# A chunked scan feeding a two-layer network: other places for weight loads, rows, pairs, dummies and state decay

## The chip, the cores and the metric

The kernel runs on one core of a Trainium2 chip. A core has five engines that run side by side and wait for one another through semaphores: TensorE (PE, matrix products into PSUM), VectorE (DVE), ScalarE (ACT), GpSimd (POOL) and SyncE (SP), which here issues every DMA. Each engine works through its own instructions in the order in which the program gives them. The metric is the device time of one execution in microseconds (us), smaller is better.

## The reference, cut to what matters

Two stages are computed: a gated linear scan over the sequence (batch 4, 8 heads, 768 positions, head size 32, state size 16), and a network of two layers over all 3072 tokens (256 to 2048 to 256, leaky ReLU between).

```python
for c in range(nc):                                   # chunks
    cum = np.cumsum(la, axis=-1)                      # la = log of the clipped gate a
    L = np.exp(cum[:, :, :, None] - cum[:, :, None, :]) * causal
    M = np.einsum('bhin,bhjn->bhij', Cc, Bc) * L
    y = np.einsum('bhij,bhjd->bhid', M, xc) \
        + np.einsum('bhin,bhnd->bhid', Cc, state) * np.exp(cum)[..., None]
    Bx = np.einsum('bhjn,bhjd->bhjnd', Bc, xc) * decay_from_j[..., None, None]
    state = decay_full * state + Bx.sum(2)
...
h = x @ w_in                                          # x: all y, tokens by heads * head size
out = np.maximum(0.01 * h, h) @ w_out
```

The weights come in double precision and are turned into a high and a low part of single precision on the chip.

## The kernel before, in words

The scan is cut into chunks of 96 positions (the result does not depend on the chunk length). One chunk of one batch element is a unit; there are 32 units, u = 4 c + b for chunk c and batch element b.

**The prelude** loads the gates `la`, takes the logarithm, and forms cumulative sums on PE: `split_sums` gives the sums as rows (`crow`, and in three bf16 parts, `parts`), `columns` gives them as columns. Both row forms go to DRAM. `keep_warm` (L112 to 117) issues matmuls of a zero tile, the dummies: 3 at the start. The decay matrix `lt` of units 0 and 1 is made directly: `decay_mask` (L226 to 231) writes a mask into PSUM, `decay_direct` adds the sums, `decay_of` takes the exponential. `dl` and `dr` are tiles of constants and of loaded parts from which `decay_pe` makes the decay of units 2 to 15 by one matmul pair each; two memsets (L146, L147) and fills prepare them.

**The first stage** (loop at L596) runs units 0 to 15, one after another: `scores` of the next unit (L301, with one dummy ahead), `unit_out` (L378: the products of the unit, L330, and its new state, L339, then copies by ACT and POOL), `decay_pe` two units ahead, and DVE's subtract `rest`. `bns[c]` are the state operands of a chunk; `state_decay(c)` (L291) multiplies them on POOL with the decay and has to come before L339 of the chunk's first unit. It is issued at the end of the last unit (b = 3) of the chunk before. From unit 3 on each unit also does one pass of the decode of the weights.

**The decode.** A weight tile f of 16 is fetched to one of three buffers `raw` (`fetch_w`, L90), then five passes: `decode_hold`, `decode_shift`, `do_sign`, `do_low` on DVE (L425, L431, L438, L445) and, from tile 3 on, `decode_rest` (L458; for the first three tiles POOL does it, L480). ACT takes the absolute value at the beginning (L420) and makes the high part at the end (L451). `do_low(f)` is the last reader of the raw tile; it issues the load of tile f + 3 right behind itself, and that load waits for it.

**The second stage** (loop at L831) has 64 steps. In step s PE multiplies a block of 512 tokens with a tile of the first weights (`ffn_in`, L517, six matmuls), ACT applies the nonlinearity twice (L524 into `gh`, L527 in place), DVE subtracts (`ffn_low`, L530, into `gl`), and three steps later PE multiplies with the second weights (`ffn_out`, L541, twelve matmuls in two banks). `hp` has two banks, so `ffn_in` of step s waits for `gl` of step s - 2. `PASSES` says how many decode passes follow in each step.

The other 16 units run in pairs at the steps of `PAIR`: `pair_block` (L382) has the products of the pair before and the scores of the new one. Their decay goes another way: `decay_rows` (L269) loads the sums from DRAM (`crow_d`) to all partitions of `lt`, `decay_sub` (L276) subtracts on POOL, `decay_exp` (L283) takes the exponential on ACT and a causal select on POOL. The dictionary `early` holds what a step issues ahead of all else: rows four steps before the pair, subtracts three and two, exponentials two and one, the state decay one. `lt` has four buffers, so the rows of a pair wait for the products of the pair before.

**The third stage** (`two_tiles`, L762) does the last two token blocks together with seven products in place of eight. `COMBINE` is the step at which its operands begin to be formed, `LAST_OUT` the step of the last scan products.

What sets the order is the program text alone: each engine and SP's DMA queue do their instructions in that order, and a waiting instruction holds up all behind it.

Of the kernel before, what the change touches and what calls it, by code (L numbers as in the profile page):

```python
# [17 lines left out]
NB, NH, S, D, N = 4, 8, 768, 32, 16  # L18
Q = 96
# [10 lines left out]
C_COLS = NB * 2 * Q  # L30
BC_COLS = B_COLS + C_COLS
LAG = 3
WARM = 3
RAWS = 3
SHIFT = 448
LOAD = 4
# [11 lines left out]
DIRECT = 2  # L48
SLOTS = 8

PAIR = {16: 7, 18: 13, 20: 20, 22: 31, 24: 36, 26: 41, 28: 46, 30: 51}
LAST_OUT = 56
COMBINE = 57

PASSES = (3,) * 12 + (2,) * 20
KD = Q + 3 * NH + 3
MAG_MIN = float(np.uint32(0x38000000).view(np.float32))
MAG_MAX = float(np.uint32(0x47EFFFFF).view(np.float32))
# [3 lines left out]
def scan_ffn(ctx: ExitStack, tc: tile.TileContext, a_l, bc_l, bn_l, x_l, w_l, out_l):  # L62
# [27 lines left out]
    def fetch_w(f, eng=nc.sync):  # L90
        raws[f] = wr.tile([128, 2 * DM, 2], U32, name="raw")
        eng.dma_start(raws[f].rearrange("p c w -> p (c w)"), w_l[f].bitcast(U32))
# [50 lines left out]
    nc.vector.memset(later, 0.0)  # L143
    nc.vector.memset(after, 1.0)
    nc.vector.memset(less, -1.0)
    nc.vector.memset(dl[Q:], 1.0)  # L146
    nc.vector.memset(dl[Q:Q + 3 * NH, :, Q:], 0.0)  # L147
    nc.gpsimd.affine_select(
        out=upto[:, :Q], in_=upto[:, :Q], pattern=[[1, Q]], compare_op=ALU.is_ge,
        fill=0.0, base=0, channel_multiplier=-1,  # L150
# [18 lines left out]
    def fill_first():  # L169
        nc.vector.tensor_copy(dr[:Q, 0], later.unsqueeze(1).to_broadcast([Q, NH, Q]))  # L170
# [36 lines left out]
    def split_sums(prow):  # L207
        for g in range(2):
            nc.tensor.matmul(
                prow[:, g], lhsT=la[:, g * 128:(g + 1) * 128], rhs=upto[:, :Q],  # L210
                start=True, stop=True,
            )
        nc.scalar.copy(crow, prow)
        nc.vector.tensor_copy(parts[:, :, 0], prow)
        nc.vector.tensor_tensor(out=rest, in0=prow, in1=parts[:, :, 0], op=ALU.subtract)
        nc.vector.tensor_copy(parts[:, :, 1], rest)
        nc.vector.tensor_tensor(
            out=parts[:, :, 2], in0=rest, in1=parts[:, :, 1], op=ALU.subtract
        )
# [6 lines left out]
    def decay_mask(space):  # L226
        for g in range(2):
            nc.tensor.matmul(
                heads_of(space, g), lhsT=upto_b,
                rhs=later.unsqueeze(1).to_broadcast([Q, NH // 2, Q]), start=True, stop=False,  # L230
            )
# [230 lines left out]


    passes = collections.deque()

    def settle(f=None):
        for g in list(pending) if f is None else [f] * (f in pending):
# [15 lines left out]
    def do_low(f):  # L483
        decode_low(f)
        defer(decode_high, f)
        if f < POOLED:
            defer(rest_pool, f)
        if f + RAWS < NF:
            fetch_w(f + RAWS)

    for f in range(NF):
        passes.append((decode_hold, f))
# [67 lines left out]
    with tc.tile_pool(name="ps_d", bufs=2, space=PSUM, reuse_waits="tile") as ps_d:  # L560

        def free_tile():
            return ps_d.tile([128, 2, TS], F32, name="pd")

        fill_first()
        nc.vector.tensor_scalar(
            out=la, in0=la, scalar1=1e-6, scalar2=1.0, op0=ALU.max, op1=ALU.min,
        )
        nc.scalar.activation(la, la, AF.Ln)
        pds = [free_tile() for _ in range(2)]  # L570
        second = score_tile()
        for u in range(DIRECT):
            fill_reach(u)
            decay_mask(pds[u])
        fill_less()
        split_sums(first[:, 0, :2 * Q].rearrange("p (g i) -> p g i", g=2))
        nc.sync.dma_start(parts_d.rearrange("(g r) t i -> r g t i", g=2), parts)
        decay_load(DIRECT, SLOTS)
        nc.sync.dma_start(crow_d.rearrange("(g p) i -> p g i", g=2), crow)
        columns(erev, after, AF.Exp, second[:, 0])  # L580
        state_decay(0)
        nc.scalar.copy(dl[:Q], upto_b.unsqueeze(1).to_broadcast([Q, SLOTS, QE]))
        fill_slots(1, SLOTS // 2)
        decay_direct(0, pds[0])
        decay_of(0, pds[0])
        fetch_bc(1)
        fetch_w(0)
        fetch_x(1)
        fetch_bn(1)
        fetch_w(1)  # L590
        fetch_x(2)
        scores(0)
        fill_slots(SLOTS // 2, SLOTS)
        decay_direct(1, pds[1])
        decay_of(1, pds[1])
        for u in range(FIRST_UNITS):  # L596
            if u == FIRST_UNITS - 1:
                settle()
                leads.close()
                pg = ctx.enter_context(tc.tile_pool(name="pg", bufs=LAG + 2))  # L600
                pob = ctx.enter_context(tc.tile_pool(name="pob", bufs=3))
                ffn_in(0, free_tile()[:, 0])
                ffn_act(0)
            if u + 1 < FIRST_UNITS:
                scores(u + 1, 1, u == 5)
            rest = unit_out(u, free_tile())
            v = u + 2
            if v < FIRST_UNITS:
                decay_pe(v, free_tile())
            rest()  # L610
            c, b = divmod(u, NB)
            if c + 2 <= FIRST_UNITS // NB:
                if b == 0 and c:
                    alloc_x(c + 2)
                    fetch_x(c + 2)
                if b == 2:
                    fetch_bc(c + 2)
                    if c == 0:
                        fetch_w(2)
                if b == 3:  # L620
                    fetch_bn(c + 2)
            if b == 3 and c + 1 < FIRST_UNITS // NB:
                state_decay(c + 1)
            if u == 2:
                decode_abs(0)
            if u > 2 and u < FIRST_UNITS - 1:
                decode(1)
            if u > 4:
                settle()
        ffn_low(0)  # L630
        ffn_in(1, score_tile()[:, 0])

    ps_o = ctx.enter_context(tc.tile_pool(name="ps_o", bufs=2, space=PSUM, reuse_waits="tile"))
# [9 lines left out]
    for u, b in PAIR.items():  # L643
        pair_at[b] = ((u - 2, u - 1) if u > FIRST_UNITS else (), (u, u + 1))
        for e in range(2):
            at(early, b - 4, decay_rows, u + e)
            at(early, b - 3 + e, decay_sub, u + e)
            at(early, b - 2 + e, decay_exp, u + e)
    pair_at[LAST_OUT] = ((NU - 2, NU - 1), ())
# [181 lines left out]
    for s in range(total):  # L831
        for f, args in early.get(s, ()):
            f(*args)
        n = PASSES[s] if s < len(PASSES) else 2
        if s >= AHEAD:
            ffn_in(s)
        if s:
            ffn_act(s)
        settle()
        if s:  # L840
            ffn_low(s)
        if s in pair_at:
            pair_block(*pair_at[s])
        decode(n)
        if s == COMBINE:
            open_two()
            sums(0)
            sums_split(0)
            temps = [su.tile([128, 2, TS], F32, name=n) for n in ("t12", "t34")]
            combining = combine(TWO, (px, bx, px, px), temps, rhs)  # L850
        if combining:
            next(combining, None)
        if s >= LAG:
            outs_due.append(s - LAG)
        if rested or not outs_due or steps[outs_due[0]] not in firsts or outs_due[0] == 0:
            while outs_due:
                ffn_out(outs_due.popleft())
            rested = False
        else:
            rested = True  # L860
# [48 lines left out]
```

## Time and profile before

| | |
|---|---|
| Median of 3 runs | 352.66 us (349.25 to 355.47) |
| The profiled execution | 354.02 us, its span from the first to the last instruction 352.3 us |
| Prelude and first stage | 0 to about 58 us of the span |
| Second stage | about 58 to 259 us |
| Third stage | about 259 us to the end |

Times in the profile count from the start of the span. A row of the timeline gives the start, the length, the engine, the line of the kernel, the operation, the tiles (out, then in), shapes and the count; in brackets stands how long the engine was idle before it and what ended that time. Of rows with several instructions the length is from the first start to the last end. "SPq" is the time of SP's DMA issues, "issue" is waiting that the profile puts down to nothing. Rows of the chain of work that ended last give start, length, engine, tile, line and count. Rows of windows give a stretch, its length, and the busy time and count of PE, PE's weight loads, DVE, ACT and POOL, then the granted clock, the DMA share and GB/s.

### The profile page before, as it was taken

The page shows a single profiled execution, that of the slowest core. Times are in us where ns is not written, and L with a number is a line of the kernel's source. Part 1 is how long each engine was busy: PE and PEld are TensorE (multiplying, and loading weights), DVE is VectorE, ACT ScalarE, POOL GpSimd, SP SyncE. Part 2 cuts the span into 40 slices and gives each one's busy share as a digit, 9 for nine tenths or more (in the row PEclk, how much of TensorE's full clock was granted, in tenths as well). Part 3 has the DMA queues.
Part 4 walks back from the last instruction along what each step waited for, and adds up shares of the span by engine and source line. Part 5 has one row for each costly group of instructions (what it writes and reads, how often), then busy time and mean ns, then how long its engine had stood idle before and what let it go on. Part 6 is the DMA issues. An engine that isn't in the chain of part 4 may idle for free.

```text
span 352.3 us, 6257 instructions
## 1 busy us (share of the span) xinstructions
PE 329.3 (93%) x2410; PEld 252.2 (72%) x2410; DVE 206.9 (59%) x344; ACT 182.4 (52%) x354; POOL 124.4 (35%) x213
## 2 busy tenths in 40 slices
PE   8997978959699999999998999999999999999995
PEld 4554546738578778888886888788887777778774
DVE  5467557769476589443343432526747866676652
ACT  4365437475454466363526545345637564545651
POOL 4157455060340351043525445204206544466100
PEclk9999689969969999999999999999999999999999
DMA  4797321715711471011056120100001000000003
GB/s 153 223 278 213 110 97 61 219 38 188 211 62 61 139 243 40 0 37 45 0 177 180 66 79 2 61 0 0 2 0 60 2 0 0 0 3 1 0 2 119
DMA packets 10555, 27.94 MB, mean 79 GB/s; under 512 B 2109, under 2 KB 2461, under 8 KB 10525
## 3 DMA queue, kind: packets, MB, share of 16 engines
q1 hardware_dynamic: 10525, 27.54, 24.7%
q8 instruction: 19, 0.31, 0.4%
q14 instruction: 11, 0.09, 0.1%
HBM read 24.14 MB, written 3.39 MB: 78 GB/s over the span
## 4 chain that ended last, share of the span: by engine, by line
PE 72%; DVE 9%; DMA 6%; POOL 4%; issue 4%; ACT 3%; SPq 1%; POOLq 0%; ACTq 0%; DVEq 0%
PE hp L517 19%; PE op L541 19%; PE sc L723 8%; DMA lt<-crow_d 6%; PE sc L742 6%; PE op L742 3%; PE hp L723 3%; PE sc L394 2%; PE sc L311 2%; PE sc L330 2%; PE pd L330 2%; POOL lt L277 2%; DVE u L803 2%; DVE c L804 2%; PE pd L254 2%
## 5 line engine op out<-in xcount | busy, mean ns | idle before, releaser
L530 DVE TENSOR_TENSOR gl<-hp,gh 128x512 fp32r<-128x512 f32 x62 | 42.7, 689 | 81.7 <-ACT hp L527 81.6
L524 ACT ACTIVATE gh<-hp 128x512 fp32r<-128x512 f32 x62 | 36.8, 594 | 63.3 <-PE hp L517 63.2
L517 PE MATMUL hp<-xh,wh 128*128 128x512 f32 x124 | 50.0, 403 | 9.8 <-DVE gl L530 9.8
L541 PE MATMUL op<-gh,wh 128*128 128x512 f32 x128 | 51.0, 399 | 0.0
L541 PE MATMUL op<-gh,wl 128*128 128x512 f32 x128 | 49.9, 390 | 0.0
L541 PE MATMUL op<-gl,wh 128*128 128x512 f32 x128 | 49.8, 389 | 0.0
L517 PE MATMUL hp<-xl,wh 128*128 128x512 f32 x124 | 49.3, 397 | 0.0
L517 PE MATMUL hp<-xh,wl 128*128 128x512 f32 x124 | 49.2, 397 | 0.0
L366 POOL COPY xs<-stage 16x64 f32<-16x64 f32 x112 | 29.6, 264 | 42.3 <-ACT stage L363 31.3
L277 POOL TENSOR_TENSOR lt<-lt,ccol 112x768 f32<-112x768 f32 x16 | 23.5, 1469 | 51.4 <-DMA lt<-crow_d 51.3
L527 ACT ACTIVATE hp<-hp 128x512 f32<-128x512 f32 x62 | 36.7, 593 | 0.0
L517 PEld LDWEIGHTS hp<-xh,wh 128*128 128x128 f32 x124 | 23.8, 192 | 17.0 <-DVE gl L530 10.5
L689 POOL TENSOR_TENSOR sl<-s,sh 128x512 fp32r<-128x512 f32 x8 | 10.4, 1300 | 67.7 <-ACT sh L688 67.7
L541 PEld LDWEIGHTS op<-gh,wh 128*128 128x128 f32 x128 | 24.1, 188 | 7.1 <-issue 1.2
L286 POOL TENSOR_SCALAR_AFFINE_SELECT lt<-lt 96x768 f32<-96x768 f32 x16 | 14.7, 916 | 38.4 <-ACT lt L285 38.4
L541 PEld LDWEIGHTS op<-gl,wh 128*128 128x128 f32 x128 | 24.0, 188 | 5.2
L541 PEld LDWEIGHTS op<-gh,wl 128*128 128x128 f32 x128 | 24.2, 189 | 4.7
L517 PEld LDWEIGHTS hp<-xl,wh 128*128 128x128 f32 x124 | 23.8, 192 | 5.1
L517 PEld LDWEIGHTS hp<-xh,wl 128*128 128x128 f32 x124 | 23.9, 192 | 4.7
L285 ACT ACTIVATE lt<-lt 112x768 f32<-112x768 f32 x16 | 13.5, 842 | 23.5 <-POOL lt L277 23.5
L755 DVE TENSOR_TENSOR gl<-c,gh 128x512 fp32r<-128x512 f32 x24 | 24.4, 1038 | 1.4 <-ACT c L752 1.1
L751 ACT ACTIVATE gh<-c 128x512 fp32r<-128x512 f32 x24 | 15.1, 627 | 14.6 <-DVE c L804 9.1
(161 smaller groups left out, 633.8 us busy)
## 6 DMA issues: line engine op xcount, KB each, us to landing
raw<-w_l SPq DMA_DIRECT2D x16, 512.0 KB, 3.7
lt<-crow_d SPq DMA_DIRECT2D x16, 336.0 KB, 4.9
bc<-bc_l SPq DMA_DIRECT2D x8, 608.0 KB, 4.3
xs<-x_l SPq DMA_DIRECT2D x8, 384.0 KB, 7.1
out_l<-ob SPq DMA_DIRECT2D x12, 256.0 KB, 2.0
bn<-bn_l SPq DMA_DIRECT2D x8, 231.0 KB, 6.5
parts_d<-parts SPq DMA_DIRECT2D x1, 144.0 KB, 1.9
la<-a_l SPq DMA_DIRECT2D x1, 96.0 KB
```

The source lines that it names most:

```text
L277: nc.gpsimd.tensor_tensor(out=lts[u], in0=lts[u], in1=ccol[:, u * NH:(u + 1) * NH].unsqueeze(2).to_broadcast([QE, NH, Q]), op=ALU.subtract,)
L286: nc.gpsimd.affine_select(out=lt[:Q], in_=lt[:Q], pattern=[[0, NH], [1, Q]], compare_op=ALU.is_ge, fill=0.0, base=0, channel_multiplier=-1,)
L366: nc.gpsimd.tensor_copy(to[:, :, hh], stage[hh * D:hh * D + N])
L517: nc.tensor.matmul(hp, lhsT=w_half[half][:, f, k * 128:(k + 1) * 128], rhs=x[t][:, k, :], start=(n == 0), stop=(n == 5),)
L524: nc.scalar.activation(ghs[s], hp, AF.Prelu, alpha=0.01)
L527: nc.scalar.activation(hps[s], hps[s], AF.Prelu, alpha=0.01)
L530: nc.vector.tensor_tensor(out=gls[s], in0=hps.pop(s), in1=ghs[s], op=ALU.subtract)
L541: nc.tensor.matmul(op, lhsT=w_half[half][:, f, DM + m * 128:DM + (m + 1) * 128], rhs=x, start=(first and i == 0), stop=(last and i == 2),)
L723: nc.tensor.matmul(bank, lhsT=w[h], rhs=x[g], start=start and i == 0, stop=i == 2, skip_group_check=True,)
L742: nc.tensor.matmul(outs[t][m], lhsT=w_half[half][:, f, DM + m * 128:DM + (m + 1) * 128], rhs=x, start=first and i == 0, stop=last and i == 2,)
L751: nc.scalar.activation(gh, h, AF.Prelu, alpha=0.01)
L755: nc.vector.tensor_tensor(out=gl, in0=g, in1=gh, op=ALU.subtract)
```

## The change

- Weight loads: `do_low` only notes the tile; the noted loads are issued at the head of the next step (behind what `early` issues), or, in the first stage, at the end of the next unit ahead of that unit's decode pass.
- Pairs: the steps become 6, 12, 18, ... 48 (before 7, 13, 20, 31, 36, 41, 46, 51), the last products 54 (56), the combining 56 (57). Rows are loaded five steps ahead of a pair (four).
- Passes: three for 14 steps (12), but one at a step with a pair.
- Dummies: six at the start (three), two after the sums; none ahead of the scores in unit 0.
- State decay of chunk c + 1 after the third unit of chunk c (after the fourth).
- The prelude: the two memsets of `dl` move behind the sums, the fill of `dr` behind the direct reach, the masks behind the columns; the state operands of chunk 1 are fetched ahead of its x.
- In unit 0 the products come ahead of the scores of unit 1; in unit 15 `ffn_low(0)` comes right behind `ffn_act(0)`.

```diff
-WARM = 3
+WARM = 6
+WARM2 = 2
...
-PAIR = {16: 7, 18: 13, 20: 20, 22: 31, 24: 36, 26: 41, 28: 46, 30: 51}
-LAST_OUT = 56
-COMBINE = 57
-
-PASSES = (3,) * 12 + (2,) * 20
+PAIR = {16: 6, 18: 12, 20: 18, 22: 24, 24: 30, 26: 36, 28: 42, 30: 48}
+LAST_OUT = 54
+COMBINE = 56
+
+PASSES = (3,) * 14 + (2,) * 20
...
-    nc.vector.memset(dl[Q:], 1.0)
-    nc.vector.memset(dl[Q:Q + 3 * NH, :, Q:], 0.0)
...
     passes = collections.deque()
+    fetches = collections.deque()
+
+    def fetch_more():
+        while fetches:
+            fetch_w(fetches.popleft())
...
         if f + RAWS < NF:
-            fetch_w(f + RAWS)
+            fetches.append(f + RAWS)
...
-        fill_first()
...
         for u in range(DIRECT):
             fill_reach(u)
-            decay_mask(pds[u])
+        fill_first()
         fill_less()
         split_sums(first[:, 0, :2 * Q].rearrange("p (g i) -> p g i", g=2))
+        nc.vector.memset(dl[Q:], 1.0)
+        nc.vector.memset(dl[Q:Q + 3 * NH, :, Q:], 0.0)
...
         columns(erev, after, AF.Exp, second[:, 0])
+        for u in range(DIRECT):
+            decay_mask(pds[u])
+        keep_warm(second[:, 1], WARM2)
         state_decay(0)
...
         fetch_w(0)
+        fetch_bn(1)
         fetch_x(1)
-        fetch_bn(1)
...
                 ffn_act(0)
+                ffn_low(0)
+            if u == 0:
+                rest = unit_out(u, free_tile())
             if u + 1 < FIRST_UNITS:
-                scores(u + 1, 1, u == 5)
-            rest = unit_out(u, free_tile())
+                scores(u + 1, int(u > 0), u == 5)
+            if u:
+                rest = unit_out(u, free_tile())
...
-            if b == 3 and c + 1 < FIRST_UNITS // NB:
+            if b == 2 and c + 1 < FIRST_UNITS // NB:
                 state_decay(c + 1)
+            fetch_more()
...
-        ffn_low(0)
         ffn_in(1, score_tile()[:, 0])
...
-            at(early, b - 4, decay_rows, u + e)
+            at(early, b - 5, decay_rows, u + e)
...
         for f, args in early.get(s, ()):
             f(*args)
-        n = PASSES[s] if s < len(PASSES) else 2
+        fetch_more()
+        n = 1 if s in pair_at else PASSES[s] if s < len(PASSES) else 2
```

## The prediction, made before the changed kernel had run

> **What bounds the kernel now.** I read the page first, then the list of idle stretches of TensorE (PE), then the timeline around each, then who waited for whom on the queues.
>
> ```profile
> span 352.3 us, 6257 instructions
> ...
> PE 329.3 (93%) x2410; PEld 252.2 (72%) x2410; DVE 206.9 (59%) x344; ACT 182.4 (52%) x354; POOL 124.4 (35%) x213
> ...
> PEclk9999689969969999999999999999999999999999
> ```
>
> PE is the bound, and by its share of busy time there seems to be nothing left to win. The clock row says otherwise: in three places the granted clock falls to 0.6 or 0.8, so part of the 329.3 busy us is the same work done slowly. All three follow an idle stretch. The first two stretches lie in the first stage (16 units of the scan, one chunk of four units after another). Each row below is the score matmul that opens a unit, from the timeline of PE:
>
> ```profile
> 29.83 0.74 PE L311 MATMUL sc<-bc 32*112 32x192 f32 x8
> 31.77 0.59 PE L311 MATMUL sc<-bc 32*112 32x192 f32 x8
> ...
> 35.26 0.44 PE L339 MATMUL pd<-xs,bn 112*32 112x32 f32 x16 [2.42 <-POOL bn L292]
> ...
> 36.88 1.00 PE L311 MATMUL sc<-bc 32*112 32x192 f32 x8
> ...
> 40.06 1.00 PE L311 MATMUL sc<-bc 32*112 32x192 f32 x8
> ...
> 42.58 0.59 PE L311 MATMUL sc<-bc 32*112 32x192 f32 x8
> ...
> 44.84 0.74 PE L311 MATMUL sc<-bc 32*112 32x192 f32 x8
> ...
> 50.09 1.00 PE L311 MATMUL sc<-bc 32*112 32x192 f32 x8
> ...
> 52.70 0.59 PE L311 MATMUL sc<-bc 32*112 32x192 f32 x8
> ```
>
> An undisturbed unit takes 31.77 - 29.83 = 1.94 us. The unit from 31.77 takes 5.11, because the state matmul L339 waits for POOL's state decay L292, which stands behind POOL's other work of the unit before. The next two take 3.18 and 2.52: the same eight score matmuls need 1.00 us instead of 0.59, so the clock has fallen. The pattern repeats at 44.84 (5.25, then 2.61).
>
> In the second stage (steps of the feed-forward, with a scan pair every few steps) PE idles four times for over 0.7 us near a pair, and the queues tell why:
>
> ```profile
> 74.24 0.80 PE L517 MATMUL hp<-xh,wh 128*128 128x512 f32 x1 [4.41 <-DVE gl L530]
> 96.91 0.80 PE L517 MATMUL hp<-xh,wh 128*128 128x512 f32 x1 [2.72 <-DVE gl L530]
> 123.37 0.50 PE L517 MATMUL hp<-xh,wh 128*128 128x512 f32 x1 [0.77 <-DVE gl L530]
> 188.19 0.50 PE L517 MATMUL hp<-xh,wh 128*128 128x512 f32 x1 [0.95 <-DVE gl L530]
> ```
> ```profile
> 65.01 0.85 SPq L272 DMA_DIRECT2D lt<-crow_d x2
> 70.14 1.47 POOL L277 TENSOR_TENSOR lt<-lt,ccol 112x768 f32<-112x768 f32 x1 [11.25 <-DMA lt<-crow_d]
> 71.64 0.84 ACT L285 ACTIVATE lt<-lt 112x768 f32<-112x768 f32 x1 [4.89 <-POOL lt L277]
> ```
> ```profile
> SPq L92 <- DVE w L445: 75.5, 13, 10.6
> ```
>
> Read these from the bottom up. SP sends transfers in program order. A weight load L92 waits on SP until DVE has finished the decode pass that frees its buffer, 75.5 us in all, and whatever stands behind it waits too. So the rows L272 of the first pair leave only at 65.01 and land just ahead of POOL's subtract at 70.14; ACT, in order too, sits 4.89 us before the exponential L285 with the activations of the next step behind it; DVE gets no gl; PE gets no free bank and idles 4.41 us. PE names DVE, but the cause is the place of a DMA in SP's queue.
>
> **The change, part by part.**
>
> *State decay one unit sooner (b == 2).* The decay of chunks 1 to 3 moves ahead of one unit's four POOL copies and, for chunks 2 and 3, of one weight subtract.
>
> ```profile
> L292 POOL TENSOR_TENSOR bn<-bn,erev x7: 1052/1055/1060, 6.8 to 170.8; 112x512 f32<-112x512 f32 x7
> ```
>
> Its 1.05 us must then end within a unit and a half before L339 needs it. It could wait for its own transfer: behind it on POOL would stand the copies of the next unit, which nothing reads for four units. I take both stalls as gone. The five units above took 5.11 + 3.18 + 2.52 + 5.25 + 2.61 = 18.67 us. With no stall each costs between 1.94 and 2.26 (42.58 to 44.84, with a short wait in it); DVE has a decode pass in each, so I take 2.1: 18.67 - 10.5 = **8.2 us won** (ends 7.4 and 9.0).
>
> *Rows at b - 5, weight loads issued at the head of the next step, pairs every six steps.* Rows now go out one step after the pair before (the earliest at which their buffer is free) and stand ahead of the step's weight load in SP's queue, not behind it. For the first pair they are emitted two steps sooner, directly behind the load of the last first-stage decode.
>
> ```profile
> DMA to landing us min/median/max: 4.0/4.9/7.3
> ```
> ```profile
> 81.95 1.36 PE hp L517 x6
> ...
> 126.08 0.86 PE sc L394 x16
> ```
>
> (The first row is for L272.) A step is two groups of six matmuls, 2 x 1.36 = 2.72 us. From a pair's matmuls to the exponential four steps on lie more than three steps, 8.2 us; the longest landing of 7.3 and a subtract of 1.47 make 8.8, and the two banks of hp give about a step more. So all four idle stretches should go: 4.41 + 2.72 + 0.77 + 0.95 = **8.85 us won**. The slow clock behind the first two goes with them:
>
> ```profile
> 74.24 2.93 PE hp L517 x6
> 77.17 1.58 PE sc L394 x16
> 78.75 3.20 PE op L541 x12
> ...
> 96.91 2.93 PE hp L517 x6
> ...
> 101.70 1.57 PE sc L394 x16
> ```
>
> First: (2.93 - 1.36) + (1.58 - 0.86) + (3.20 - 2.72) = 2.77. Second: 1.57 + 0.71 = 2.28. Together **5.05 us won**; the work of a pair itself is not less, only placed elsewhere. The weight load a step later costs SP nothing by itself: SP runs ahead of the engines and was waiting for the same decode pass anyway, so the load leaves when that pass ends, unless the rows ahead of it wait (for the products of the pair before, past by then). What is late next is DVE. The first fourteen steps have three decode passes (one where a pair stands), and two early pairs fall among them; POOL's subtract then runs beside DVE:
>
> ```profile
> 62.50 0.68 DVE L458 TENSOR_TENSOR wl<-w,wh 128x512 fp32r<-128x512 f32 x1
> ...
> 134.44 1.74 DVE L458 TENSOR_TENSOR wl<-w,wh 128x512 fp32r<-128x512 f32 x1
> ```
> ```profile
> 80.00:94.00 14.00, 14.00 (x63) 11.41 (x61) 10.92 (x21) 5.91 (x11) 1.19 (x1) 1.00 0.74 240
> ```
>
> With almost no POOL work DVE is busy 10.92 of 14.00 us at three passes, and one pass stretched by 1.06 us beside POOL's subtract. Two pairs with two subtracts each give 4 x 1.06 = 4.2 us of DVE time; between 0 and 4.2 of it reaches PE, and I take **2 us lost**. (The Trainium skill, "SBUF — State Buffer", Who interferes with whom, says that a DVE instruction with two SBUF inputs is blocked for the whole of a GpSimd instruction that reads SBUF. By that rule each subtract could hold DVE for its full 1.47 us, 5.9 in all; the trace shows 1.06 at the worst place I found.)
>
> *gl of step 0 moved into unit 15.* In the trace PE waits for it:
>
> ```profile
> 58.61 0.47 PE L517 MATMUL hp<-xh,wh 128*128 128x512 f32 x1 [0.97 <-DVE gl L530]
> ```
>
> It now goes ahead of the unit's own subtract on DVE. **0.5 won** (0 to 0.97).
>
> *The prelude: three dummies more at the start, two before the decay of chunk 0, masks behind the sums, no dummy in unit 0.*
>
> ```profile
> 1.06 1.46 PE L114 MATMUL sc<-idle 128*128 128x512 bf16 x3 [1.06 <-DVE idle L110]
> 3.08 1.53 PE L228 MATMUL pd<-later,upto_b 96*112 96x384 bf16 x4 [0.56 <-DVE upto_b L192]
> 6.08 2.77 PE L235 MATMUL pd<-lt,after 96*112 96x384 f32 x4
> 14.90 0.89 PE L254 MATMUL pd<-dr,dl 123*112 123x384 bf16 x2
> 17.99 0.53 PE L254 MATMUL pd<-dr,dl 123*112 123x384 bf16 x2
> ```
>
> Six dummies at 1.46 / 3 = 0.49 end near 4.0, in time that PE spent on the masks or idle, so they cost nothing. The four mask matmuls (1.53) lay in the shadow of the logarithm and now stand on PE's path, with 2 x 0.49 of dummies; one dummy goes (0.5), and the sums start perhaps 0.4 sooner: 1.53 + 0.98 - 0.5 - 0.4 = 1.6 later at the slow clock, half of that if the clock rises at the same time. I take **1.2 lost**. The ends are 3.3 lost (the rise falls a stretch of slow clock later as well) and about 4 won (second rival). The moved memsets and fills of DVE and the swapped transfers bn and x of chunk 1 have later readers and count zero; cover gone, they cost their own length, under 1 us each. An end of the scan two steps sooner, combining one step sooner: zero, as the third stage waits for none of it.
>
> **Sum:** -8.2 - 8.85 - 5.05 - 0.5 + 2 + 1.2 = -19.4. The profiled execution took 354.02 us around its span of 352.3, which gives 334.6; it stands 1.36 above the median of 352.66, from which the sum gives 333.3. The slow stretches differ between executions and most of them should go, so I also count a little for what I left out (the slow products at the second stall): **333 us**.
>
> **The rivals.**
>
> 1. *One pair still stalls, or DVE becomes the bound.* For it: DVE's 78% at three passes, before POOL's share; the loads of a chunk now share DMA with rows and weights. Against: the median landings. One stall as large as the first keeps 4.41 + 2.77 = 7.2: 340. All 4.2 us of the stretched passes: 335 to 336.
>
> 2. *The dummies raise the clock early.* If the clock rises near 8 instead of between 14.90 and 17.99, ten us of slow work halve at most; ScalarE and DVE between the units leave some 4: 333 - 1.2 - 4 = 328. Against:
>
> ```profile
> 3.08:14.90 11.82, 11.82 (x67) 6.49 (x67) 6.56 (x12) 4.50 (x7) 2.76 (x3) 1.00 0.56 181
> ```
>
> PE is busy for all 11.82 us from 3.08 on, and still the two L254 matmuls take 0.89 at 14.90 and 0.53 only at 17.99; the long fp32 matmuls (L235) seem not to count as full activity, and they stay behind the dummies. The Trainium skill, "TensorE: Matmul & The Clock Gate", Part 1, gives some 3.4 us of sustained work as enough, in a free-running window. Taken plainly that rule speaks for this rival, but the trace does not agree with it here, as 11.82 us without a gap did not do.
>
> 3. *The pairs do not move off the path.* If the rows are held by something other than the weight loads, the second stage keeps its 13.9 us: 347, about no change.
>
> 4. *Slower: weights arrive late.* Ten weight tiles are loaded in the loop. Behind rows and a chunk's transfers each may land late, ACT's absolute value of the tile waits, and the activations wait behind it, as they did for L285.
>
> ```profile
> DMA to landing us min/median/max: 3.1/3.7/9.7
> ```
>
> Between the pass that frees a buffer and the pass that needs its next tile lie nine passes and three gl on DVE, 12 x 10.92 / 21 = 6.2 us. At the median of 3.7 it is 2.5 early; at 9.7 it would be 3.5 late. To end over 2% slower all ten would have to cost (19.4 + 7) / 10 = 2.6 us, so nearly every landing beyond 8.8. Nothing in the trace comes near that.
>
> **How the numbers follow.** 329 to 337 us, as forecast: 0.45. Second rival, 325 to 329: 0.13; below that 0.02. First rival, 337 to 342: 0.22. Between this and the third (342 to 347): 0.10. Other small gains or none, to 359: 0.05. Fourth rival, beyond 359.7: 0.03. From 325 to 342 lie 0.80. Two per cent, about what a measurement of this kernel can tell from no change, is 7 us: faster than 345.6 is 0.89 (0.07 of the 0.10), within 0.08, slower 0.03.
>
> **What would show it.** Right: no L339 waiting for L292 over 0.5 us, and units near 2.1 us up to the feed-forward; no fall of the clock after the prelude; L272 issued right after a pair's products; no gl wait on PE over 1 us. The prelude's step is wrong if the L254 of unit 2 or earlier takes 0.53. The forecast is wrong if PE still waits for gl near the first two pairs, with L285 waiting for L277 (rows late), or with DVE busy without a gap (DVE the bound), or with the absolute value L420 waiting for a weight transfer (fourth rival).

## The result, and the profile after

| | median | runs | lowest to highest |
|---|---|---|---|
| Before (beside the changed kernel) | 352.54 us | 11 | 350.90 to 356.68 |
| Changed | 333.58 us | 5 | 332.60 to 333.99 |

The ratio is 0.9462, with a 95% interval of 0.9438 to 0.9486: 19.0 us less. An earlier set of four runs gave a ratio of 0.9506 (0.9361 to 0.9652), in which one execution of 788.77 us does not count. Every matmul of the feed-forward is twice as long there; it stands in the last section, and the profile after shown here is of another execution (332.69 us, span 331.0).

The page of the changed kernel:

```profile
span 331.0 us, 6272 instructions
...
PE 315.6 (95%) x2414; PEld 244.3 (74%) x2414; DVE 217.1 (66%) x344; ACT 182.9 (55%) x354; POOL 126.6 (38%) x213
...
PEclk9999999999999999999999999999999999999999
```

PE is busy 13.7 us less although it has four more matmuls: the clock no longer falls. This is not peculiar to the two profiles: the mean granted clock was 0.969 to 0.984 in the eleven executions of before and 0.993 to 1.000 in the five of the changed kernel. To see where the rest went, set the starts of the units against those of before. First one row of before, then the timeline of PE after (start, length, engine, line, tiles, and in brackets the wait ahead):

```profile
16.15 1.00 PE L311 MATMUL sc<-bc 32*112 32x192 f32 x8
```
```profile
12.19 0.50 PE L254 MATMUL pd<-dr,dl 123*112 123x384 bf16 x2 [1.33 <-DMA dr<-parts_d]
12.85 0.59 PE L311 MATMUL sc<-bc 32*112 32x192 f32 x8
...
29.06 0.59 PE L311 MATMUL sc<-bc 32*112 32x192 f32 x8
...
32.15 0.38 PE L116 MATMUL sc<-idle 128*128 128x512 bf16 x1 [1.18 <-DVE lt L318]
32.46 0.74 PE L311 MATMUL sc<-bc 32*112 32x192 f32 x8
...
36.19 0.74 PE L311 MATMUL sc<-bc 32*112 32x192 f32 x8
...
38.46 0.74 PE L311 MATMUL sc<-bc 32*112 32x192 f32 x8
...
40.91 0.38 PE L116 MATMUL sc<-idle 128*128 128x512 bf16 x1 [0.65 <-DVE lt L318]
...
43.16 0.59 PE L311 MATMUL sc<-bc 32*112 32x192 f32 x8
...
48.36 0.51 PE L522 MATMUL hp<-xh,wh 128*128 128x512 f32 x1 [0.25 <-DVE gl L535]
...
56.36 0.50 PE L522 MATMUL hp<-xh,wh 128*128 128x512 f32 x1 [0.59 <-DVE gl L535]
...
63.86 0.50 PE L522 MATMUL hp<-xh,wh 128*128 128x512 f32 x1 [2.26 <-DVE gl L535]
```

The first row of L311 here is unit 2, then come units 9, 10, 12, 13 and 15. With the rows of before in the prediction this gives, stage by stage:

| stretch | before | after | difference |
|---|---|---|---|
| start to the scores of unit 2 | 16.15 | 12.85 | -3.30 |
| units 2 to 8 | 15.62 | 16.21 | +0.59 |
| the five units that held both state-decay stalls (9 to 11, 13, 14) | 18.67 | 7.13 + 4.70 = 11.83 | -6.84 |
| unit 12 | 2.26 | 2.27 | +0.01 |
| unit 15 to the feed-forward | 5.91 | 5.20 | -0.71 |
| second stage | 205.74 | 194.64 | -11.10 |
| third stage | 87.95 | 88.0 | 0 |

The second stage is read from windows (the stretch and its length, then the busy time and count of PE, PE's weight loads, DVE, ACT, POOL, the granted clock, the DMA share, GB/s), of before and of after:

```profile
58.61:264.35 205.74, 196.88 (x1341) 158.33 (x1341) 116.09 (x192) 105.81 (x207) 61.43 (x95) 0.97 0.25 79
```
```profile
48.36:63.86 15.50, 12.63 (x65) 9.41 (x65) 14.88 (x22) 11.59 (x22) 7.28 (x8) 1.00 0.48 154
63.86:243.00 179.14, 179.14 (x1277) 145.28 (x1277) 110.98 (x172) 95.36 (x187) 57.01 (x89) 1.00 0.25 79
```

(A step has six matmuls of L522 and six of L546, two times three; a row with twelve of them spans two steps.) Before, PE was idle for 205.74 - 196.88 = 8.86 us. After, it is idle for 2.87, all in the first 15.5 us, and from 63.86 on it does not stop once in 179 us. The other 5.11 us (196.88 - 12.63 - 179.14) are the same count of matmuls (1341) done at a fuller clock, 0.97 before and 1.00 after. The two profiles differ by 21.3 us and the medians by 19.0: the profile of before stands 1.5 above its median here, that of after 0.9 below.

The cause that the prediction named, the place of the rows in SP's queue, is seen in the first issue of L272 after:

```profile
46.46 0.84 SPq L272 DMA_DIRECT2D lt<-crow_d  x2
```
```profile
52.36 1.47 POOL L277 TENSOR_TENSOR lt<-lt,ccol 112x768 f32<-112x768 f32 x1 [2.90 <-DMA lt<-crow_d]
```

The feed-forward begins at 48.36, so the rows of the first pair now leave 1.9 us ahead of it; before they left at 65.01, 6.4 us behind 58.61.

### The profile page after: what moved, and what is told of

It is laid out like the page before. It is cut to its first block, busy times and chain, and to the rows that moved or that the text cites. A ratio compares the mean times of both kernels' runs of the same rounds, so it can differ in the third digit from the quotient of the medians.

```text
span 787.1 us, 6272 instructions
## 1 busy us (share of the span) xinstructions
PE 782.1 (99%) x2414; PEld 457.4 (58%) x2414; DVE 210.7 (27%) x344; ACT 184.4 (23%) x354; POOL 118.6 (15%) x213
## 4 chain that ended last, share of the span: by engine, by line
PE 99%; DVE 0%; ACT 0%; issue 0%
PE op L546 29%; PE hp L522 28%; PE sc L736 9%; PE sc L755 7%; PE op L755 7%; PE hp L736 4%; PE sc L311 2%; PE sc L394 2%; PE pd L330 2%; PE sc L330 2%; PE pd L254 2%; PE sc L116 2%; PE pd L235 1%; PE pd L339 1%; PE sc L339 0%; PE sc L522 0%
## 5 line engine op out<-in xcount | busy, mean ns | idle before, releaser
L546 PE MATMUL op<-gh,wh 128*128 128x512 f32 x128 | 107.6, 841 | 0.0
L546 PE MATMUL op<-gh,wl 128*128 128x512 f32 x128 | 105.2, 822 | 0.0
L546 PE MATMUL op<-gl,wh 128*128 128x512 f32 x128 | 105.2, 822 | 0.0
L522 PE MATMUL hp<-xl,wh 128*128 128x512 f32 x124 | 104.0, 838 | 0.0
L522 PE MATMUL hp<-xh,wl 128*128 128x512 f32 x124 | 103.0, 831 | 0.0
L522 PE MATMUL hp<-xh,wh 128*128 128x512 f32 x124 | 101.6, 819 | 0.0
L546 PEld LDWEIGHTS op<-gl,wh 128*128 128x128 f32 x128 | 45.6, 357 | 31.3 <-issue 30.8
L546 PEld LDWEIGHTS op<-gh,wl 128*128 128x128 f32 x128 | 45.8, 358 | 30.5 <-issue 30.5
L546 PEld LDWEIGHTS op<-gh,wh 128*128 128x128 f32 x128 | 43.8, 342 | 32.4 <-issue 31.4
L522 PEld LDWEIGHTS hp<-xh,wh 128*128 128x128 f32 x124 | 43.9, 354 | 31.1 <-issue 26.5
L522 PEld LDWEIGHTS hp<-xl,wh 128*128 128x128 f32 x124 | 43.0, 347 | 29.2 <-issue 28.5
L522 PEld LDWEIGHTS hp<-xh,wl 128*128 128x128 f32 x124 | 43.3, 349 | 28.5 <-issue 28.5
L366 POOL COPY xs<-stage 16x64 f32<-16x64 f32 x112 | 29.8, 266 | 143.4 <-ACT stage L363 120.6
L736 PE MATMUL sc<-xl,sh 128*128 128x512 f32 x32 | 26.7, 835 | 0.0
L755 PE MATMUL sc<-gl,wh 128*128 128x512 f32 x32 | 26.6, 832 | 0.0
L755 PE MATMUL op<-gh,wl 128*128 128x512 f32 x32 | 26.6, 831 | 0.0
```

The lines of the kernel that those rows point to most:

```text
L366: nc.gpsimd.tensor_copy(to[:, :, hh], stage[hh * D:hh * D + N])
L522: nc.tensor.matmul(hp, lhsT=w_half[half][:, f, k * 128:(k + 1) * 128], rhs=x[t][:, k, :], start=(n == 0), stop=(n == 5),)
L546: nc.tensor.matmul(op, lhsT=w_half[half][:, f, DM + m * 128:DM + (m + 1) * 128], rhs=x, start=(first and i == 0), stop=(last and i == 2),)
L736: nc.tensor.matmul(bank, lhsT=w[h], rhs=x[g], start=start and i == 0, stop=i == 2, skip_group_check=True,)
L755: nc.tensor.matmul(outs[t][m], lhsT=w_half[half][:, f, DM + m * 128:DM + (m + 1) * 128], rhs=x, start=first and i == 0, stop=last and i == 2,)
```

## Experiments: the two halves of the scan's stalls

Times are medians of five or six runs, ratios to the kernel before, run beside it.

**decay_late**: the changed kernel, with the state decay a unit later again.

```diff
-            if b == 2 and c + 1 < FIRST_UNITS // NB:
+            if b == 3 and c + 1 < FIRST_UNITS // NB:
                 state_decay(c + 1)
```

> The changed kernel with the state decay back after the fourth unit of a chunk. My theory puts 8.2 us on this term (7.4 to 9.0): 342 to 344 us if the changed kernel takes 334.8, with two waits of L339 for L292 of about 2.4 us and the clock falling behind each. A rival in which PE would have idled there for its transfers or for VectorE anyway expects 0 to 3 us more.

339.50 us, ratio 0.9660 (0.9616 to 0.9704): 5.9 us more. The timeline of PE has the stalls back, and slow units behind them:

```profile
32.12 0.33 PE L339 MATMUL pd<-xs,bn 112*32 112x32 f32 x16 [1.82 <-POOL bn L292]
...
33.27 0.99 PE L311 MATMUL sc<-bc 32*112 32x192 f32 x8
...
44.05 0.45 PE L339 MATMUL pd<-xs,bn 112*32 112x32 f32 x16 [2.42 <-POOL bn L292]
```

The mechanism holds. The size is 5.9 and not 8.2, below the range given, mostly because the units that lost this stall gained another (32.15 and 40.91 above, 1.83 us together, which the profile of decay_late does not have). Where that one comes from stands under rest_later.

**second_old**: the changed kernel with the whole second stage of before (loads, rows, pairs and passes as they were).

```diff
-PAIR = {16: 6, 18: 12, 20: 18, 22: 24, 24: 30, 26: 36, 28: 42, 30: 48}
-LAST_OUT = 54
-COMBINE = 56
...
+PAIR = {16: 7, 18: 13, 20: 20, 22: 31, 24: 36, 26: 41, 28: 46, 30: 51}
+LAST_OUT = 56
+COMBINE = 57
+PASSES = (3,) * 12 + (2,) * 20
...
-            fetches.append(f + RAWS)
+            fetch_w(f + RAWS)
...
-            at(early, b - 5, decay_rows, u + e)
+            at(early, b - 4, decay_rows, u + e)
...
-        n = 1 if s in pair_at else PASSES[s] if s < len(PASSES) else 2
+        n = PASSES[s] if s < len(PASSES) else 2
```

> The changed kernel with the whole second stage of before: loads with the decode pass, rows four steps ahead, pairs at 7, 13, 20, 31, 36, 41, 46, 51, three passes in the first twelve steps and none less beside a pair. Prelude and first stage stay as changed. If the stages add up, it takes the 333.58 us of the changed kernel and the 11.1 us that its second stage was shorter by: 343 to 346. If a first stage that ends sooner and at a full clock takes the stalls of the second stage with it (they were longer for a slow clock ahead of them), it takes less: 337 to 341. PE's waits for gl at the first two pairs (4.41 and 2.72 us before) say which.

343.56 us, ratio 0.9742 (0.9694 to 0.9791): 10.0 us more than the changed kernel, so the stages add up. PE's waits at the first two pairs:

```profile
64.97 0.80 PE L522 MATMUL hp<-xh,wh 128*128 128x512 f32 x1 [4.69 <-DVE gl L535]
...
88.98 0.80 PE L522 MATMUL hp<-xh,wh 128*128 128x512 f32 x1 [4.94 <-DVE gl L535]
```

A first stage at a full clock does not shorten them: they were not owed to a slow start.

## Experiments: which step clears the queue

Three steps of the change touch the second stage's queue. Each was undone or done alone, then two together. The numbers of decode passes in each step were not undone alone.

**loads_at_once**: loads issued with the decode pass again.

```diff
-            fetches.append(f + RAWS)
+            fetch_w(f + RAWS)
```

> The changed kernel with the weight loads issued at once, in the decode pass that frees their buffer, and the rows still five steps ahead. My theory holds that SP's queue order is what counts: with rows a step sooner than before and pairs elsewhere, only a few rows still stand behind a waiting load. I expect 0 to 5 us more than the changed kernel. A theory by which the later loads are the heart of the second stage's gain expects 9 to 14 us more, with waits of ScalarE L285 for GpSimd L277 as before. A theory by which later loads hurt (weights late) expects 1 to 5 us less.

334.53 us, ratio 0.9483 (0.9453 to 0.9513): 0.95 us more, within the intervals no difference.

**rows_four**: rows four steps ahead again.

```diff
-            at(early, b - 5, decay_rows, u + e)
+            at(early, b - 4, decay_rows, u + e)
```

> The changed kernel with the rows four steps ahead of a pair, as before, and the rest of the change kept. My theory: what counts is what stands ahead of the rows in SP's queue. For the first pair nothing comes between the two places, for the second the chunk's three transfers and one waiting weight load do. So the rows of the second pair leave some 8 us later and ScalarE's L285 waits for GpSimd once: 0 to 3 us more than the changed kernel. A theory by which the fifth step carries the second stage's gain expects 7 us or more.

334.64 us, ratio 0.9512 (0.9459 to 0.9565): 1.1 us more, again no difference that the intervals show.

**before_loads_later**: the kernel before, with the later weight loads alone (the `fetches` queue, emptied at the head of each step and at the end of each unit).

```diff
+    fetches = collections.deque()
...
-            fetch_w(f + RAWS)
+            fetches.append(f + RAWS)
...
+            fetch_more()
...
+        fetch_more()
```

> The kernel before with one edit: the weight loads noted and issued at the head of the next step. Rows still four steps ahead, pairs at the old steps. By the queue theory the rows of the first pair now stand behind one waiting load fewer, leave about 3.7 us sooner, and the first idle stretch of 4.41 us shrinks below 1 with the slow clock behind it: 5 to 7 us less than before; the later pairs gain less. A theory by which the steps of the pairs made the difference expects no more than 1 us.

348.50 us, ratio 0.9899 (0.9847 to 0.9951): 4.2 us less than the 352.66 beside it. The first two stalls shrink from 4.41 and 2.72 to 2.91 and 1.24; a new one of 1.84 appears at 114.14, where PE waits for DVE's sum of an output, behind a decode pass that stands beside two POOL instructions (DVE, then POOL):

```profile
110.59 2.81 DVE L438 SCALAR_TENSOR_TENSOR w<-raw,w 128x512 uint32<-128x512 uint32 x1
```
```profile
110.17 1.24 POOL L286 TENSOR_SCALAR_AFFINE_SELECT lt<-lt 96x768 f32<-96x768 f32 x1 [1.91 <-ACT lt L285]
111.38 1.47 POOL L277 TENSOR_TENSOR lt<-lt,ccol 112x768 f32<-112x768 f32 x1
```

This misses what was expected: the rows of the first pair do leave about as much sooner as forecast (3.1 us behind the start of the feed-forward, before 6.4), but the first stall does not fall below 1 us. Part of the gain is also lost in the first stage, where L339 waits once more for L292 (1.08 us at 26.17).

So the later load was worth 4.2 us in one kernel and 1 in the other. Either it matters little, or each step covers for the other. The next two runs tell these apart.

**both_undone**: the two edits of loads_at_once and rows_four together.

> The changed kernel with both steps undone that were meant to get a pair's rows past the weight loads on SP: a load issued with the decode pass again, rows four steps ahead again. Pairs every six steps stay. Undone one at a time these steps cost about 1 us each (334.53 and 334.64 against 333.58). Theory A (each of the two does the other's work, so only both together are felt): at least one stall of 2.5 to 4.4 us at the first two pairs comes back with its stretch of slow clock, 338 to 344 us. Theory B (the places of the pairs carry the gain of the second stage, the two steps are worth 1 us each at most): 334.5 to 336.5 us, and no wait for gl over 2.5 us.

340.87 us, ratio 0.9681 (0.9632 to 0.9729): 7.3 us more, far beyond 0.95 + 1.1. PE waits again at the first two pairs:

```profile
60.81 0.49 PE L522 MATMUL hp<-xh,wh 128*128 128x512 f32 x1 [2.48 <-DVE gl L535]
...
83.79 0.58 PE L522 MATMUL hp<-xh,wh 128*128 128x512 f32 x1 [3.02 <-DVE gl L535]
```

And the first issue of L272 in SP's queue, in order loads_at_once, rows_four, both_undone:

```profile
45.70 0.85 SPq L272 DMA_DIRECT2D lt<-crow_d  x2
```
```profile
49.09 0.84 SPq L272 DMA_DIRECT2D lt<-crow_d  x2
```
```profile
51.62 0.85 SPq L272 DMA_DIRECT2D lt<-crow_d  x2
```

The feed-forward begins at 47.63, 50.99 and 48.21 there. With either step alone the rows leave 1.9 us ahead of it, exactly as in the changed kernel; with neither they leave 3.4 us behind. In both_undone a weight load stands directly ahead of them on SP, issued at 51.20 when its decode pass was over; in loads_at_once the rows follow the load of 45.27 and the next one leaves behind them, at 50.62. They need only get ahead of that one load. Either edit does it, and the second adds nothing at this place.

The second pair shows another side of it. Its issue of L272, in order the changed kernel, loads_at_once, rows_four, both_undone:

```profile
61.66 0.84 SPq L272 DMA_DIRECT2D lt<-crow_d  x2
```
```profile
68.81 0.84 SPq L272 DMA_DIRECT2D lt<-crow_d  x2
```
```profile
72.03 0.89 SPq L272 DMA_DIRECT2D lt<-crow_d  x2
```
```profile
72.42 1.34 SPq L272 DMA_DIRECT2D lt<-crow_d  x2
```

Counted from the start of the feed-forward these are 13.3, 21.2, 21.0 and 24.2 us. Here a single undone step does delay the rows, by almost 8 us, and yet PE does not stop at this pair: that much could be spared. With both undone ACT sits 5.57 us before L285 (2.67 and 0.50 with one), and PE idles the 3.02 us shown above. So theory A holds, and at this pair it is slack and not the same place in the queue that hides a single step.

**old_pairs**: the changed kernel with the pairs at the steps of before.

```diff
-PAIR = {16: 6, 18: 12, 20: 18, 22: 24, 24: 30, 26: 36, 28: 42, 30: 48}
-LAST_OUT = 54
-COMBINE = 56
...
+PAIR = {16: 7, 18: 13, 20: 20, 22: 31, 24: 36, 26: 41, 28: 46, 30: 51}
+LAST_OUT = 56
+COMBINE = 57
```

> The changed kernel with the pairs at the steps of before (7, 13, 20, 31, 36, 41, 46, 51; last block 56, combining at 57); loads later and rows five steps ahead stay, and one decode pass where a pair stands. Theory A (loads and rows carry the gain): 333 to 336 us, no wait for gl over 2.5 us. Theory B (the places carry it): the first two pairs stall for 1.2 to 2.9 us each as they did where only the loads of before were moved, 337 to 341 us.

335.32 us, ratio 0.9523 (0.9473 to 0.9573): 1.7 us more, at the edge of what the intervals resolve. There is no wait for gl over 1.84. The places of the pairs carry little; loads and rows carry most of the gain, 7.3 of the 10.0 us that undoing the whole second stage costs.

## Experiments: DVE beside POOL

**few_passes**: the changed kernel, with two decode passes in steps 3 to 5, where PE waited 2.26 us.

```diff
-PASSES = (3,) * 14 + (2,) * 20
+PASSES = (3,) * 3 + (2,) * 3 + (3,) * 10 + (2,) * 20
```

> The changed kernel with two decode passes rather than three in steps 3 to 5. In its profile TensorE waits 2.26 us for gl ahead of step 7, while VectorE holds a decode pass L425 for 2.13 us beside GpSimd's select and state decay. If VectorE beside GpSimd is the bound there, fewer passes ahead of that gl bring it sooner: 1 to 2 us less, and the wait under 0.8. If the wait comes from ScalarE's exponentials (L285 behind the rows), nothing changes.

331.24 us, ratio 0.9431 (0.9369 to 0.9493). The wait of 2.26 us stands behind the scores of the first pair, ahead of step 7; it falls to 0.52:

```profile
61.26 0.50 PE L522 MATMUL hp<-xh,wh 128*128 128x512 f32 x1 [0.52 <-DVE gl L535]
```

The median is 2.3 us lower, a little more than forecast, but two of the six executions took 335.3 and the intervals overlap, so it is the profile that carries this. What had happened in the changed kernel is read from DVE and POOL, between 58 and 63 us:

```profile
58.72 1.71 DVE L438 SCALAR_TENSOR_TENSOR w<-raw,w 128x512 uint32<-128x512 uint32 x1
...
61.08 2.13 DVE L425 TENSOR_SCALAR w<-w 128x512 f32<-128x512 f32 x1
63.12 0.68 DVE L535 TENSOR_TENSOR gl<-hp,gh 128x512 fp32r<-128x512 f32 x1
```
```profile
58.42 1.46 POOL L277 TENSOR_TENSOR lt<-lt,ccol 112x768 f32<-112x768 f32 x1
60.83 1.06 POOL L286 TENSOR_SCALAR_AFFINE_SELECT lt<-lt 96x768 f32<-96x768 f32 x1 [0.95 <-ACT lt L285]
61.87 1.05 POOL L292 TENSOR_TENSOR bn<-bn,erev 112x512 f32<-112x512 f32 x1
```

Two passes that take 0.68 and 0.42 alone took 1.71 and 2.13. The second began behind the select and ended 0.29 behind the state decay that followed it (63.21 against 62.92): DVE did not get in between the two POOL instructions. gl had to wait for it, and PE for gl.

**rest_later**: few_passes, with POOL's weight subtract a unit later in the first stage, so that it no longer follows the state decay directly.

```diff
+    late = collections.deque()
+
+    def rest_late():
+        while late:
+            rest_pool(late.popleft())
...
-            defer(rest_pool, f)
+            defer(late.append, f)
...
+            rest_late()
             fetch_more()
```

> The changed kernel with two decode passes in steps 3 to 5 (331.24 us alone) and, in the first stage, the weight subtract of POOL issued one unit later, so that it no longer follows the state decay directly. Theory A (DVE's decode pass took 2.30 us at 29.33 and 1.46 at 38.92 because POOL's decay and subtract stood back to back, and the two waits of PE for lt behind it, 1.18 and 0.66 us, come from that): these waits fall to under 0.4 us together, 329.4 to 330.5 us. Theory B (any POOL subtract with two operands holds DVE by its own length wherever it stands, so the wait only moves by a unit): 331 to 332 us, with waits of 0.5 to 1 us a unit later.

332.00 us, ratio 0.9418 (0.9368 to 0.9468). The median is above that of few_passes and the ratio below: no difference. The profile says more. In the changed kernel, DVE and POOL around 30 us:

```profile
29.33 2.30 DVE L425 TENSOR_SCALAR w<-w 128x512 f32<-128x512 f32 x1
31.55 0.55 DVE L318 TENSOR_TENSOR lt<-sc,lt 112x384 f32<-112x384 f32 x1
```
```profile
29.06 1.06 POOL L292 TENSOR_TENSOR bn<-bn,erev 112x512 f32<-112x512 f32 x1 [1.84 <-PE pd L254]
30.08 1.27 POOL L485 TENSOR_TENSOR wl<-w,wh 128x512 fp32r<-128x512 f32 x1
```

And in rest_later, DVE and PE:

```profile
31.20 0.46 DVE L425 TENSOR_SCALAR w<-w 128x512 f32<-128x512 f32 x1
...
33.15 1.13 DVE L431 TENSOR_SCALAR w<-w 128x512 uint32<-128x512 uint32 x1
```
```profile
20.20 0.65 PE L330 MATMUL pd<-lt,xs 112*32 112x96 f32 x15 [1.53 <-DMA xs<-x_l]
...
34.79 0.38 PE L116 MATMUL sc<-idle 128*128 128x512 bf16 x1 [0.28 <-DVE lt L318]
...
43.31 0.38 PE L116 MATMUL sc<-idle 128*128 128x512 bf16 x1 [0.40 <-DVE lt L318]
```

The pass of 2.30 us takes 0.46 once the two POOL instructions stand apart; the next pass pays 1.13 for the moved subtract. The two waits go from 1.18 + 0.65 to 0.28 + 0.40, and each stands a unit later than in the changed kernel (ahead of units 11 and 15, not 10 and 14). So each theory has a part: two POOL instructions back to back held DVE longer than they do apart, as A has it, but the subtract alone still holds a pass and the rest of the wait moves with it, as B has it. The time is B's, and A's 0.4 us for both waits is missed. In this execution PE waited 1.53 us for a transfer of x at 20.20, and a stretch of slow clock followed. These times do not show it better than few_passes.

## Experiments: the prelude

**old_prelude**: the changed kernel with the whole prelude and unit 0 of before.

```diff
+WARM = 3
...
+        fill_first()
...
             fill_reach(u)
+            decay_mask(pds[u])
...
-        keep_warm(second[:, 1], WARM2)
...
+                scores(u + 1, 1, u == 5)
+            rest = unit_out(u, free_tile())
```

> The changed kernel with the whole prelude of before (three dummies, masks ahead of the sums, memsets and fills early, x of chunk 1 ahead of its state operands, one dummy and the scores of unit 1 ahead of the products of unit 0). The prediction's sum had the new prelude lose 1.2 us, so 1.2 us less than the changed kernel. The second rival had it win: the first profiles show the clock risen near 4 us and the third group of scores at 12.85 against 16.15 before, so 3 us more, less what later waits take back; with the clock rising at 14 us or later.

335.62 us, ratio 0.9518 (0.9470 to 0.9566): 2.0 us more. All six executions (334.05 to 336.34) lie above the five of the changed kernel (332.60 to 333.99), though the intervals of the ratios touch and one of the earlier set took 337.01. The new prelude gains, where a loss of 1.2 was forecast; how much is less sure than that.

**no_dummies**: the changed kernel with three dummies at the start and none behind the sums; masks, fills and memsets as changed.

```diff
-WARM = 6
+WARM = 3
...
-        keep_warm(second[:, 1], WARM2)
```

> The changed kernel with three dummies at the start and none after the sums, otherwise as it is. My theory has the dummies raise nothing: the two after the sums cost 0.98 us at the slow clock, so 0.5 to 1 us less than the changed kernel, within the noise of single runs. The second rival (dummies raise the clock early) expects 2 to 4 us more, and L254 of units 2 and 3 at 0.89 us where the changed kernel has 0.53.

336.29 us, ratio 0.9493 (0.9442 to 0.9545), from 332.45 to 338.04: what the dummies are worth stays unresolved. The median is 2.7 us more, as the second rival expected, but L254 of unit 2 takes 0.50, as it did not. The profile is of one of the two executions near 332.5, with the same span as the changed kernel's, 331.0 us; the other four took 335.75 to 338.04, and no profile shows when the clock rose in them. The rise is read from the lengths of matmuls, since the granted clock reads 1.00 also in the slow stretch from 3.08 to 14.90. In the profiles the clock has risen by 4.72 in the changed kernel (L228 below), by 9.28 in no_dummies (scores at 0.59 us), and with the prelude of before not yet at 14.90 (L254 takes 0.89). Two rows for the same four mask matmuls, of the changed kernel and of second_old, which has the same prelude:

```profile
4.72 0.81 PE L228 MATMUL pd<-later,upto_b 96*112 96x384 bf16 x4
```
```profile
5.50 1.49 PE L228 MATMUL pd<-later,upto_b 96*112 96x384 bf16 x4
```

Once the clock had risen by then, once it had not. So the moment of the rise differs between executions of one instruction order, but in all ten profiles of the new order (without the execution of 788.77 us) the first L254 (at 11.9 to 13.8 us) takes 0.50 to 0.53, and in the three of the old order 0.89. Whether it is the masks' new place or another part of the order that does this was not separated; no_dummies shows that three dummies can be enough for it, in one execution.

## Why the prediction came out right, step by step

Forecast were 333.0 us and a sum of 19.4 us won; 333.58 came, 19.0 us less between the medians and 21.3 between the two profiles. The total is closer than its terms:

| term of the sum | forecast | undone alone | from the two profiles |
|---|---|---|---|
| state decay a unit sooner | -8.2 | -5.9 | -6.84 |
| second stage (idle -8.85, slow clock -5.05, DVE +2) | -11.9 | -10.0 | -11.10 |
| gl of step 0 | -0.5 | not tried alone | -0.71 |
| prelude | +1.2 | -2.0 | -3.30, of which +0.59 is lost again in units 2 to 8 |

*State decay: right in mechanism, mis-sized.* In the profile after, L339 waits for L292 nowhere, as asked. The margin is thin: with the same or almost the same first stage it waits 0.6 us once in rows_four and in both_undone. The step that failed is "with no stall each costs between 1.94 and 2.26". Units 9 and 13 took 3.40 and 2.75, since the decay now runs directly ahead of POOL's weight subtract and the two hold a DVE pass for 2.30 and 1.46 us. The prediction counted that contention for the pairs of the second stage and not for the unit to which it moved the decay. It wrote that the decay moves "ahead of one unit's four POOL copies and, for chunks 2 and 3, of one weight subtract", and had the collision in that sentence.

*Second stage: right in mechanism, near in both terms.* The slow clock gave 5.11 against 5.05. Of the 8.85 us of idle time 5.99 went, against 8.85 - 2 = 6.85: "two pairs with two subtracts each ... I take 2 us lost" was 2.87. One sign named for "right" failed with it, "no gl wait on PE over 1 us": one of 2.26 is left. This is the first rival's "DVE becomes the bound", in a small dose: DVE is busy for 14.88 of the first 15.50 us. Its sum was set up on a stretch of 1.06 us for one pass beside one subtract. The pass that hurt most stood beside a select and a state decay, 1.71 us longer than alone, and these two were not in the sum. The Trainium skill, "SBUF — State Buffer", Who interferes with whom, describes an exclusive lock, held for a whole instruction, that can also reach one-input `tensor_scalar` forms. The rows agree (L425 is one), and go on to show a pass held through two POOL instructions that follow one another.

*What clears the queue.* The prediction gave the loads, the rows and the pairs one common price. The price was about right (-11.9, and -11.1 between the profiles). What it did not say is that loads and rows are substitutes (1 us each undone alone, 7.3 together) and that the pairs' places are worth 1.7 in the medians, barely clear of the noise.

*Prelude: wrong in sign.* The step that failed is the term "1.2 lost", and with it the argument against the second rival, that 11.82 us without a gap had not raised the clock. They had not in that order of instructions; with the new order it rose within 4 to 10 us. The sign named for this ("L254 of unit 2 or earlier takes 0.53") is there: 0.50 at 12.19. By its price that rival forecast 328 us; of the 4 us that it had the prelude win, 2.0 reach the median. That its dummies are the cause is not shown. In the profiles the scores of unit 2 stand 3.3 us ahead of old_prelude's, behind a new wait of 1.33 for `dr` (12.19); at unit 9 the lead is 2.6 (29.06 against 31.64), as a wait of 0.89 in unit 8 has come in, and at the feed-forward 2.3 (48.36 against 50.64). The Trainium skill, "TensorE: Matmul & The Clock Gate", Part 1, has the rise after one window of 3.4 us in which PE is busy, at a phase that differs from run to run. That it had risen by 4.72 in one profile and not by 5.50 in another of the same prelude agrees; why the old order takes over 14 us is not explained by it.

*The other rivals.* The third (no gain from the queue) and the fourth (weights late) did not happen. From 63.86 us to the end of the second stage PE waits for nothing.

So a miss of 2.3 in the state decay, about 2 in the second stage and 3.2 the other way in the prelude nearly cancelled. That 333 was met within 0.6 us is luck; that the two large terms have the right cause and about the right size is not.

## What to carry to other kernels

Before two fixes for one stall are priced one by one, ask whether either suffices: undo them singly and together, or each will look worthless. When an instruction is moved next to another on the same engine, look at what the two as a block hold up on another engine (here DVE beside POOL), not at each alone. A stall's gain includes the slow clock behind it, here 5.11 of the second stage's 11.10 us.

## What the runs showed of the hardware

- A decode pass of DVE (L425 to L445) that began while a subtract, a select or a state decay ran on POOL waited out that instruction, all but two of 165 in the thirteen profiles (the execution of 788.77 us not counted). Where a second one followed within 0.1 us, in 42 of these, it waited out that one too, each time. The two `TENSOR_SCALAR` passes shown ended 0.28 us (31.63 against 31.35) and 0.29 us (63.21 against 62.92) behind the last of two. The `SCALAR_TENSOR_TENSOR` pass shown ended 0.55 us behind it (113.40 against 112.85) and took 2.81 us in place of 0.68. POOL's small copies (L366) do not hold a pass: one beside four of them took 0.42 us (48.49, profile after).
- One execution of the changed kernel took 788.77 us. Its page:

```profile
span 787.1 us, 6272 instructions
...
PE 782.1 (99%) x2414; PEld 457.4 (58%) x2414; DVE 210.7 (27%) x344; ACT 184.4 (23%) x354; POOL 118.6 (15%) x213
...
L546 PE MATMUL op<-gh,wh 128*128 128x512 f32 x128 | 107.6, 841 | 0.0
```

  The same group in the profile after:

```profile
L546 PE MATMUL op<-gh,wh 128*128 128x512 f32 x128 | 50.5, 395 | 0.0
```

  DVE, ACT and POOL are busy for about as long as in the profile after; PE alone is slow, over the whole span, while the granted clock reads 1.00. It was seen once in all these runs, and its cause is open.
- In the first stage PE stops for 0.6 to 1.6 us amid the products L330 of one to three units, at a place that moves between kernels (0.64 us at 24.00 before, 0.89 at 27.79 after, 1.59 at 24.22 in old_prelude). The profile names "issue", a POOL copy or a transfer for it. What it is stays open.
